# A transposed tile's source moved out of the product buffers, one layernorm reordered and one attention step put a unit later, in a two-layer transformer kernel

## The chip, the cores and the metric

The kernel runs on one core of a Trainium2 chip. The metric is the time on the device in microseconds (us); lower is better. The profiler's span is about 1.7 us shorter than the timed run it belongs to (1243.4 against 1245.1 us for the profile of before), so spans are compared with spans and times with times.

Names of engines: PE is TensorE (matmuls), DVE is VectorE, ACT is ScalarE, POOL is GpSimd, SP issues most of the transfers. The granted clock is the share of TensorE's full clock that the chip let it have, in a stretch of time or as the mean of a run. PSUM is where the matmuls write their results (the `psum` tiles of the kernel), `rstd` is one over a row's standard deviation, and the zero halo is a block of zeros that stands in for the rows above the first.

## The reference

Two layers, each an attention block and a dense block, on x of 2048 rows and 1024 columns in bfloat16:

```python
x = x + A(layernorm(x))     # qkv; attention; @ wo
x = x + B(layernorm(x))     # gelu(x @ w1 + b1) @ w2 + b2
x = x + A(layernorm(x))
x = x + B(layernorm(x))
```

The attention has 32 heads of 32 columns. Each row looks at eight rows only: itself and those 2, 4, ... 14 above it. So the logits are no matmul of q with k: VectorE multiplies q with eight shifted views of k, and a matmul with a matrix of ones and zeros sums the products over each head's columns (a "head sum").

## The kernel before

The rows are worked in four groups of 512. A group's layernorm output `xn` is transposed into `xnT`, on PE for group 0 and by transfers (DMA transposes) for the others. Then come q, k and v in eight chunks of columns each. One chunk is eight matmuls and is called a unit here: units 0 to 7 make q, 8 to 15 make k, 16 to 23 make v. Work that belongs to other stages is hung in at a numbered unit (`sides=at(unit, ...)`).

The part that matters is the start, where the rotation of buffers is filled for the first time. Everything named "big" shares three buffers of 8 KB per partition: the warm-up operand, `xn` of groups 1 and 2, and then the products of q and k.

```python
bigp = ctx.enter_context(tc.tile_pool(name="bigp", bufs=3))
...
def ln_early(n, pool=None):           # layernorm of groups 1 and 2
    xa[n] = new_xnT(pool)
    xns = bigp.tile([P, NTT, D], BF16, name="big")
    ...
        ln_norm(n * NTT + tt, *s[tt], xns[:, tt, :])
        sp.dma_start_transpose(xa[n][:, tt, :, :], xns[:, tt, :]...)
...
def new_prod(n, c):                   # q times shifted k, then pairwise sums
    prod = bigp.tile([P, W, T], BF16, name="big")
    vec.tensor_tensor(out=prod[:], in0=s["qT"]..., in1=win(s["kT"]...), op=ALU.mult)
    ... # after every second product: add two; after every fourth: once more
...
def ln_first():                       # layernorm of group 0
    stats[0] = ln_stats(0)
    stats[1] = ln_stats(1)
    norm(0)
    norm(1)
    stats[2] = ln_stats(2)
    stats[3] = ln_stats(3, between=lambda: norm(2))  # norm(2) between its halves
    norm(3)
...
stage(gen_qkv(0, 2, qk_next=early), sides=... + at(21, head_sum, 0, False))
q1 = gen_qkv(1, 2, defer=True, qk_pool=early)
stage(q1, sides=at(5, attend, 0) + at(5, spread, 0) + at(5, hold) + ...)
```

Group 0 has two head sums. The first (`head_sum(0, False)`, unit 21 of group 0's stage) sums the first four products. The second is the first act of `attend(0)` at unit 5 of group 1's stage: it sums the other four, and the softmax follows. PE takes its instructions in this fixed order, so it waits at a head sum if VectorE is late.

## Time and profile before

| | before |
|---|---|
| time, median of four runs (lowest to highest) | 1243.96 us (1243.51 to 1246.25) |
| the run that the profile shows | 1245.1 us, span 1243.4 us |
| PE busy | 1235.0 us, 99% |
| PE idle, all of it | 8.4 us |

From the page of before, the span, the row of PE's busy time and the shares of the chain that ended last:

```profile
span 1243.4 us, 14103 instructions
PE 1235.0 (99%) x5871; PEld 633.6 (51%) x5871; DVE 836.8 (67%) x864; ACT 305.9 (25%) x477; POOL 94.1 (8%) x215
...
PE 96%; DVE 2%; DMA 1%; SPq 1%; issue 0%; POOL 0%; DVEq 0%
```

PE is the bound, so only its idle time and its slow time can be won. The waits of PE in before (who waited for whom: us in total, times, longest):

```profile
PE L L118 <- DVE big L93: 2.7, 1, 2.7
PE acc L118 <- DVE big L93: 1.1, 1, 1.1
PE acc L118 <- ACT xnT L93: 0.7, 1, 0.7
PE L L217 <- ACT xnT L93: 0.5, 1, 0.5
PE acc L217 <- POOL rstd L93: 0.2, 1, 0.2
```

The longest is one wait of 2.7 us of a head sum (its result is the tile `L`) for the products. The next view, PE's timeline of before, has the columns start, duration, engine, line, operation, tiles, shapes, count and, in brackets, the idle time before and what ended it:

```profile
37.56 12.31 PE L118 MATMUL acc<-xnT,wt 128*128 128x512 bf16 x56
52.58 0.61 PE L118 MATMUL L<-big,smat 128*32 128x512 bf16 x8 [2.72 <-DVE big L93]
53.13 15.72 PE L118 MATMUL acc<-xnT,wt 128*128 128x512 bf16 x64
68.78 0.61 PE L118 MATMUL L<-big,smat 128*32 128x512 bf16 x8
```

The two head sums are at 52.58 and 68.78 us. VectorE's timeline of before shows why the first is late. The third product starts after a wait of 6.33 us for the transposes that read the `xn` in its buffer:

```profile
34.77 2.29 DVE L93 TENSOR_TENSOR big<-big 128x4096 bf16<-128x4096 bf16 x1
43.38 4.50 DVE L93 TENSOR_TENSOR big<-qT,kT 128x4096 bf16<-128x4096 bf16 x2 [6.33 <-DMA xnT<-big]
47.91 4.62 DVE L93 TENSOR_TENSOR big<-big 128x4096 bf16<-128x4096 bf16 x2
...
63.89 4.62 DVE L93 TENSOR_TENSOR big<-big 128x4096 bf16<-128x4096 bf16 x2
```

The last line is the last addition for the second head sum. It ends at 68.51 us, and PE's second head sum starts at 68.78.

The windows view of before gives the busy time of each engine (with its number of instructions), then the granted clock, the share of the DMA engines and GB/s:

```profile
50.00:53.40 3.40, 0.82 (x9) 0.32 (x9) 3.37 (x3) 0.49 (x1) 0.00 (x0) 1.00 1.05 395
53.40:56.80 3.40, 3.40 (x9) 1.34 (x8) 3.40 (x2) 0.15 (x1) 0.00 (x0) 0.50 0.22 82
56.80:60.00 3.20, 3.20 (x16) 2.16 (x15) 3.06 (x3) 1.59 (x4) 0.00 (x0) 1.00 0.36 58
```

From 53.4 to 56.8 us PE works at half clock. Its busy time alone does not show that: it is 3.40 of 3.40 us, but with 9 matmuls in place of about 17. This agrees with the Trainium skill ("Trainium Kernel Development and Optimization", Performance Expectations), which calls the busy time of matmuls a bad metric for how close a kernel is to its roofline.

A smaller stall lies in the first layernorm. ScalarE's timeline of before:

```profile
13.37 0.29 ACT L93 COPY kT<-zhalo 128x112 bf16<-128x112 bf16 x1 [3.21 <-POOL zhalo L93]
13.56 0.28 ACT L93 COPY vT<-zhalo 128x112 bf16<-128x112 bf16 x1
13.75 1.00 ACT L93 COPY xnT<-L 128x1024 bf16<-128x1024 bf16 x1
```

and PE's, at the same place:

```profile
12.34 0.61 PE L217 MATMUL L<-ident,xn 128*128 128x128 bf16 x8
...
14.80 0.61 PE L217 MATMUL L<-ident,xn 128*128 128x128 bf16 x8 [0.53 <-ACT xnT L93]
```

The transposes of tile 2 were done at 12.95 us, but ScalarE stood before a copy of a zero block that GpSimd wrote only at 13.15 us, behind the `rstd` of tile 3. The transposes of tile 3 then waited 0.53 us for ScalarE. The Trainium skill ("TensorE: Matmul & The Clock Gate", Part 1) calls the queues of ScalarE, VectorE and GpSimd strictly first in, first out. The trace agrees: the copy out of `L` starts at 13.75 us, after the two copies of zeros, though its input was ready 0.8 us earlier.

### The profile page before, as it was taken

To read this page: it belongs to the slowest core of one execution; us is meant where nothing else is said; L and a number is where in the kernel's file an instruction comes from. 1 tells how busy PE (TensorE), PEld (TensorE's weight loads), DVE (VectorE), ACT (ScalarE), POOL (GpSimd) and SP (SyncE) were. 2 spreads that over 40 slices of the span, in tenths; PEclk is the share of its full clock that TensorE was granted. 3 is DMA by queue.
4 is the path that set the end of the run, shared out by engine and by line. 5 is a ranking of instruction groups with operands and counts; after the bars stand their busy time and mean duration, and the time that the engine had idled before them with its cause. 6 is when DMAs were issued, how large, how long until landed. Compare 5 with 4: busy or idle time off the path is not lost.

```text
span 1243.4 us, 14103 instructions
## 1 busy us (share of the span) xinstructions
PE 1235.0 (99%) x5871; PEld 633.6 (51%) x5871; DVE 836.8 (67%) x864; ACT 305.9 (25%) x477; POOL 94.1 (8%) x215
## 2 busy tenths in 40 slices
PE   9999999999999999999999999999999999999998
PEld 6566544456444564445644456444554444444444
DVE  7799889996995889427994379943598688012001
ACT  3333152013430134201351013410234101310310
POOL 4010111002001100101000010000000002000000
PEclk9999999999999999999999999999999999999999
DMA  9863564485746557655566565566754567546441
GB/s 283 268 210 138 153 207 148 161 199 182 218 129 205 167 155 201 190 170 147 177 173 197 166 179 166 161 201 194 192 160 141 182 203 196 164 156 195 147 138 55
DMA packets 215328, 219.83 MB, mean 177 GB/s; under 512 B 66066, under 2 KB 184992, under 8 KB 212192
## 3 DMA queue, kind: packets, MB, share of 16 engines
q1 hardware_dynamic: 212592, 208.16, 55.9%
q0 software_dynamic: 2672, 10.76, 2.7%
q8 instruction: 46, 0.75, 0.2%
q14 instruction: 18, 0.15, 0.0%
HBM read 197.40 MB, written 6.29 MB: 164 GB/s over the span
## 4 chain that ended last, share of the span: by engine, by line
PE 96%; DVE 2%; DMA 1%; SPq 1%; issue 0%; POOL 0%; DVEq 0%
PE acc L118 95%; DVE big L93 1%; DVE stats L93 1%; DMA x<-in_A_x_dram 1%; SPq L93 1%; PE L L118 0%; DMA xnT<-big 0%; POOL rstd L93 0%; DVE mv L93 0%; PE acc L217 0%; DVE x L93 0%; DVEq L93 0%
## 5 line engine op out<-in xcount | busy, mean ns | idle before, releaser
L118 PE MATMUL acc<-xnT,wt 128*128 128x512 bf16 (+1 forms) x3376 | 724.1, 377 | 0.7 <-ACT xnT L93 0.7
L118 PEld LDWEIGHTS <-wt 128*128 128x128 bf16 x3376 | 398.4, 119 | 322.4 <-issue 6.4
L118 PE MATMUL acc<-wt,hT 128*128 128x512 bf16 (+1 forms) x1820 | 388.1, 376 | 0.0
L118 PEld LDWEIGHTS <-hT 128*128 128x128 bf16 x1820 | 178.2, 98 | 208.9
L93 DVE TENSOR_TENSOR big<-big 128x2048 bf16<-128x2048 bf16 (+2 forms) x182 | 239.5, 1348 | 1.7
L93 ACT ACTIVATE hT<-acc,b1T 128x512 bf16<-128x512 f32 x224 | 151.6, 687 | 318.5 <-PE acc L118 317.8
L93 DVE TENSOR_TENSOR big<-abc,vT 128x4096 bf16<-128x4096 bf16 x64 | 143.9, 2282 | 49.2 <-DMA abc<-a_d 48.8
L93 DVE TENSOR_TENSOR big<-qT,kT 128x4096 bf16<-128x4096 bf16 x64 | 143.8, 2286 | 30.4 <-ACT kT L93 23.4
L93 DVE TENSOR_TENSOR tmp<-acc,b2bc 128x512 f32<-128x512 f32 x56 | 38.7, 691 | 177.7 <-PE acc L118 173.9
L93 ACT CAST qT<-acc 128x512 bf16<-128x512 f32 x64 | 37.2, 585 | 326.4 <-PE acc L118 326.4
L118 PE MATMUL acc<-wt,oT 128*128 128x512 bf16 x448 | 97.9, 379 | 0.0
L93 DVE BATCH_NORM_STATS2 stats<-x 128x6 f32<-128x512 bf16 x128 | 84.1, 678 | 3.7 <-DMA x<-in_A_x_dram 2.7
L118 PEld LDWEIGHTS <-oT 128*128 128x128 bf16 x448 | 43.8, 98 | 52.9 <-issue 0.2
L93 DVE TENSOR_TENSOR x<-acc,big 128x512 bf16<-128x512 f32 (+1 forms) x9 | 5.7, 632 | 90.0 <-PE acc L118 90.0
L93 ACT CAST vT<-acc 128x512 bf16<-128x512 f32 x64 | 37.5, 586 | 89.3 <-PE acc L118 89.3
L93 ACT CAST kT<-acc 128x512 bf16<-128x512 f32 x64 | 37.5, 585 | 73.0 <-PE acc L118 73.0
L93 POOL TENSOR_TENSOR rstd<-mv,eps_t 128x1 f32<-128x1 f32 x60 | 16.2, 270 | 502.5 <-DVE mv L93 502.5
L93 POOL DMA_DIRECT2D a_d<-a x32 | 18.9, 619 | 411.0 <-DVE a L93 411.0
L93 DVE TENSOR_SCALAR xn<-x,mv,rstd 128x1024 bf16<-128x1024 bf16 x52 | 28.7, 551 | 31.3 <-POOL rstd L93 30.3
L93 DVE TENSOR_TENSOR x<-acc,x 128x512 bf16<-128x512 f32 x64 | 43.0, 672 | 6.7 <-PE acc L118 6.5
L93 DVE TENSOR_TENSOR x<-tmp,x 128x512 bf16<-128x512 f32 x56 | 38.7, 691 | 1.7
L93 POOL TENSOR_TENSOR rstd<-rstd,mhalf 128x1 f32<-128x1 f32 x60 | 33.9, 565 | 4.7
(55 smaller groups left out, 215.6 us busy)
## 6 DMA issues: line engine op xcount, KB each, us to landing
wt<-in_B_w_dram SPq DMA_DIRECT2D x56, 1024.0 KB, 5.8
wt<-in_B_w_dram SPq DMA_DIRECT2D x64, 896.0 KB, 4.9
wt<-in_A_wqkv_dram SPq DMA_DIRECT2D x46, 1024.0 KB, 5.5
wt<-in_A_wo_dram SPq DMA_DIRECT2D x16, 1024.0 KB, 5.0
abc<-a_d POOLq DMA_DIRECT2D x32, 256.0 KB, 4.8
x<-in_A_x_dram SPq DMA_DIRECT2D x16, 256.0 KB, 6.2
out_dram<-x SPq DMA_DIRECT2D x31, 128.0 KB, 1.8
wt<-in_A_wqkv_dram SPq DMA_DIRECT2D x4, 512.0 KB, 7.7
```

The lines of the kernel that those rows point to most:

```text
L93: inst = f(*args, **kwargs)
L118: return pe(nc.tensor.matmul(*args, **kwargs))
```

## The change

The intent: the third group's `xn` (group 2) takes the room of the second group's `qT`, which is not written until PE works on group 1, so that no product waits for group 2's transposes. The first layernorm computes both statistics before it normalises tiles 2 and 3. And `attend(0)` comes one unit later.

```diff
-    def ln_stats(t, mv=None, rstd=None, between=None):
+    def ln_stats(t, mv=None, rstd=None):
 ...
-            if h == 0 and between is not None:
-                between()
 ...
-        stats[3] = ln_stats(3, between=lambda: norm(2))
+        stats[3] = ln_stats(3)
+        norm(2)
         norm(3)
 ...
-        xns = bigp.tile([P, NTT, D], BF16, name="big")
+        xns = bigp.tile([P, NTT, D], BF16, name="big") if pool is None else pool.tile([P, NTT, D], BF16, name="qT")
 ...
-        stage(q1, sides=at(5, attend, 0) + at(5, spread, 0) + at(5, hold) + ...
+        stage(q1, sides=at(6, attend, 0) + at(6, spread, 0) + at(6, hold) + ...
```

## The prediction

> **What bounds the kernel now.** TensorE. The page gives PE 99% busy (1235.0 of 1243.4 us); the chain that ended last is 96% PE. By the timeline, PE's 8.4 us of idle time lies in the first 53 us (1.05 at the start, 0.22, 0.67, 0.53, 2.72) and in a tail of 3.2 us; between them PE never stands still.
>
> **Stall A, 2.72 us, from 49.86.** PE waits for VectorE's first products of group 0 before the first head sum. VectorE is late because its third product waited 6.33 us (37.05 to 43.38) for a product buffer: the waits view says "DMA xnT<-big", the transposes of the third group's xn, which lies in one of the three product buffers. The chain of waits passes through it.
> Afterwards the windows view gives a granted clock of 0.50 from 53.4 to 56.8 us. The casts of vT, otherwise 1.73 us apart, show the eight matmuls after the stall taking 3.45 us and the next eight 1.88: about 1.8 us more lost. The Trainium skill ("TensorE: Matmul & The Clock Gate", Part 1) has PE fall to half clock after an idle window of about 3.4 us and return after a busy one. The trace agrees in length (3.4 us at 0.50), but 2.72 us of idle were enough.
>
> **Stall B, 0.53 us, at 14.27.** The transposes of tile 3 wait for ScalarE's copy of tile 2 out of PSUM. It could have started at about 13.0, but ScalarE's queue first held a copy of the zero halo, which GpSimd wrote only at 13.15, behind the rstd of tile 3, behind VectorE's split statistics.
>
> **What the change does.**
> 1. xn of group 2 moves into the room of group 1's qT, not written before about 55 us; its transposes land by 42.9. The third product then needs only the room of group 1's xn, long transposed, and starts at about 37.1. What ended at 52.5 ends at about 46.2; PE comes at about 49.3. Stall A goes, and its slow clock: -2.72 and -1.8.
> 2. norm(2) ends about 0.35 us later (11.8; PE wants it at 12.2), but tile 3's statistics 0.9 us earlier. The zero halo comes at about 12.3, the PSUM copy ends at about 14.05: stall B goes, -0.5. The next statistics still start at about 13.8, when x lands.
> 3. Attend 0 one unit (1.73 us) later: PE reaches it at about 65.4, not 68.8; VectorE's last add ends at about 62.2, not 68.5. No PE wait; some 4 us idle on VectorE. Softmax and AV of group 0 run 3.4 us earlier, done at about 124.1; PE's wo starts at about 126.7, not 131.8. Slack falls from 4.3 to 2.6 us: still no stall. From the residual adds on, VectorE follows PE, so the whole gain stays.
>
> No work is removed or added; durations stay. All of the gain is on PE's chain: 2.72 + 1.8 + 0.53, about 5.0 us.
>
> **Prediction: 1238.9 us, range 1237.5 to 1241.5.** Faster by over 2%: 1%; within 2%: 98%; slower by over 2%: 1%.
>
> **What would show it.** PE's 2.7 us wait before L gone; no granted clock under 1.0 after 50 us; VectorE's 6.3 us wait on "xnT<-big" gone; PE idle 3.2 to 3.5 us less; span about 1238.4.
>
> **What would make it wrong.** The third product waiting for another buffer (1 to 2 us of stall left); VectorE late at wo or at the late transposes, giving back 1 to 2 us; stall B merely moving; the slow clock returning.

## The result, and the profile after

The changed kernel took 1239.95 us (median of four runs, 1239.72 to 1239.99) against 1243.96 us of before. The ratio is 0.9964, with a 95% interval of 0.9946 to 0.9981. A ratio here is taken over the runs of the same rounds, so it is not quite the ratio of the medians quoted. The gain is 4.0 us in the medians; the two profiled spans differ by 5.2 us.

The page of after:

```profile
span 1238.2 us, 14051 instructions
PE 1230.7 (99%) x5821; PEld 632.5 (51%) x5871; DVE 836.5 (68%) x864; ACT 305.9 (25%) x477; POOL 95.9 (8%) x215
...
PE 99%; issue 0%; ACT 0%; DVE 0%
```

(The 50 matmuls that PE has less are records missing from the trace: the weight loads are 5871 in both, and the two programs have the same number of instructions on PE.) All waits of PE in after:

```profile
PE acc L118 <- DVE big L93: 1.1, 1, 1.1
PE acc L118 <- ACT xnT L93: 0.7, 1, 0.7
```

Both waits, for the head sum and for `xnT` out of `L`, are gone; what is left is the very start and the 0.7 us at 9 us. (The 0.2 us for `rstd` is gone too, but that is no work of the change: this wait runs from nothing to 1.0 us in the profiles, and e5, which has the same layernorm as after, shows the 1.0.) PE's timeline of after has both head sums without a wait, the first 3.6 us earlier:

```profile
48.97 0.62 PE L118 MATMUL L<-big,smat 128*32 128x512 bf16 x8
49.51 15.76 PE L118 MATMUL acc<-xnT,wt 128*128 128x512 bf16 x72
65.20 0.61 PE L118 MATMUL L<-big,smat 128*32 128x512 bf16 x8
```

VectorE's timeline of after: three products in a row from 29.98 us, no wait, the first half sum done at 45.92, the last addition at 61.90, and then 4.21 us of idle time before the softmax:

```profile
29.98 6.69 DVE L93 TENSOR_TENSOR big<-qT,kT 128x4096 bf16<-128x4096 bf16 x3
...
41.30 4.62 DVE L93 TENSOR_TENSOR big<-big 128x4096 bf16<-128x4096 bf16 x2
...
57.28 4.62 DVE L93 TENSOR_TENSOR big<-big 128x4096 bf16<-128x4096 bf16 x2
66.11 1.22 DVE L93 TENSOR_REDUCE mx<-L 128x128 f32<-128x1024 f32 x1 [4.21 <-PE L L118]
```

The windows view of after, the stretch that ran at half clock in before:

```profile
53.40:56.80 3.40, 3.40 (x18) 2.26 (x16) 3.40 (x2) 1.69 (x5) 0.00 (x0) 1.00 0.94 301
```

Twice the matmuls in the same time, at full clock. In the first layernorm, ScalarE's copy out of `L` now starts at 12.85 us and PE's last transposes have no wait:

```profile
12.85 1.01 ACT L93 COPY xnT<-L 128x1024 bf16<-128x1024 bf16 x1
```
```profile
13.97 0.61 PE L215 MATMUL L<-ident,xn 128*128 128x128 bf16 x8
```

### The profile page after: what moved, and what is told of

The parts are those of the page before. It is cut to its first block, busy times and chain, and to the rows that moved or that the text cites. A ratio compares the mean times of both kernels' runs of the same rounds, so it can differ in the third digit from the quotient of the medians.

```text
span 1238.2 us, 14051 instructions
## 1 busy us (share of the span) xinstructions
PE 1230.7 (99%) x5821; PEld 632.5 (51%) x5871; DVE 836.5 (68%) x864; ACT 305.9 (25%) x477; POOL 95.9 (8%) x215
## 4 chain that ended last, share of the span: by engine, by line
PE 99%; issue 0%; ACT 0%; DVE 0%
PE acc L118 99%; PE L L118 0%; PE acc L215 0%; PE L L215 0%; ACT xnT L93 0%; DVE x L93 0%; DVE big L93 0%; PE acc L185 0%
```

## The experiments

Eleven kernels ran. All gave the right result. They went in three batches, each on one chip with nine runs of before beside it, and each kernel was timed in five runs:

| run | what it is | median us (lowest to highest) | ratio to before (95% interval) |
|---|---|---|---|
| batch 1 | before, nine runs | 1243.90 (1243.13 to 1244.64) | |
| e1_before_again | before, unchanged | 1243.86 (1243.32 to 1244.26) | 0.9998 (0.9984 to 1.0011) |
| e2_buffer_only | before + xn in qT's room | 1240.25 (1240.18 to 1240.94) | 0.9971 (0.9959 to 0.9984) |
| e3_norm_only | before + norm(2) later | 1244.11 (1243.17 to 1245.24) | 1.0001 (0.9989 to 1.0014) |
| e4_attend_only | before + attend at unit 6 | 1242.42 (1241.57 to 1244.26) | 0.9990 (0.9977 to 1.0002) |
| batch 2 | before, nine runs | 1244.16 (1242.98 to 1245.24) | |
| e5_after_attend5 | after, attend at unit 5 | 1240.05 (1239.75 to 1240.41) | 0.9968 (0.9954 to 0.9981) |
| e6_halo_early | e2 + zero block written first | 1239.84 (1239.73 to 1240.30) | 0.9967 (0.9954 to 0.9979) |
| e7_before_filled | before + 7 idle-time matmuls | 1244.06 (1243.88 to 1245.35) | 1.0002 (0.9990 to 1.0015) |
| e10_attend_filled | e4 + 7 idle-time matmuls | 1242.26 (1241.56 to 1243.75) | 0.9988 (0.9975 to 1.0000) |
| batch 3 | before, nine runs | 1243.85 (1243.33 to 1244.85) | |
| e11_first_xn_moved | before, the other xn moved | 1243.88 (1242.78 to 1244.72) | 1.0000 (0.9986 to 1.0013) |
| e8_after_u18 | after, first head sum at unit 18 | 1241.83 (1241.53 to 1243.62) | 0.9985 (0.9972 to 0.9997) |
| e9_after_u17 | after, first head sum at unit 17 | 1245.85 (1243.37 to 1245.91) | 1.0010 (0.9997 to 1.0022) |

### e1_before_again: the kernel before once more

No edit. The profile of before was of a run of 1245.1 us, 1.1 us over the median, and the runs of before spread over 2.7 us where those of after lie within 0.3 us.

> The kernel before, unchanged, to see the span and granted clock of each of its runs. Theory: the 2.72 us of idle before the first head sum lets the clock fall, and how long it stays low depends on when the idle falls, so the runs spread over about 1243.4 to 1246.3 us, and a slower run has more microseconds at a clock of 0.50 after 50 us. Rival: the slow clock costs the same 1.8 us each time; then the runs lie within 0.3 us of one another, near 1245.0.

Its runs spread over 0.9 us, and the nine of before beside it over 1.5 us. That looked like the theory; its profile says otherwise. PE's timeline of e1_before_again:

```profile
51.67 0.61 PE L118 MATMUL L<-big,smat 128*32 128x512 bf16 x8 [2.27 <-DVE big L93]
52.22 14.04 PE L118 MATMUL acc<-xnT,wt 128*128 128x512 bf16 x64
67.66 0.62 PE L118 MATMUL L<-big,smat 128*32 128x512 bf16 x8 [1.40 <-DVE big L93]
```

The clock did not fall at this gap (in this trace it fell only in the tail, at 1241.09 us, when PE's last matmul was over). The 64 matmuls took 14.04 us and not 15.72. But PE did not gain by it: it came to the second head sum early and waited there 1.40 us for VectorE. The runs are not faster for having a good clock either: one at 1243.86 us had a mean clock of 0.999, one at 1244.26 us of 1.000. So a second theory was needed. In before, VectorE sets the time up to the second head sum: its third product starts when group 2's transposes have landed, and 25.13 us of products and additions later (43.38 to 68.51 us in the profile of before) PE may go on. How PE spends the time before that, idle or at half clock, hardly matters.

### e2_buffer_only: the room of qT alone

```diff
-        xns = bigp.tile([P, NTT, D], BF16, name="big")
+        xns = bigp.tile([P, NTT, D], BF16, name="big") if pool is None else pool.tile([P, NTT, D], BF16, name="qT")
```

> The kernel before with the third group's xn in the room of qT alone. Theory: the wait of 6.3 us for a product buffer, PE's stall of 2.72 us and the slow clock all go; only the 0.53 us at 14.3 us stays: 1240.5 us, 3.4 to 3.6 us under the median of before. Rival (the gain comes from attend 0 one unit later): 1243.5 to 1244.0.

It came to 1240.25 us, 3.65 us under before. The move of `xn` is nearly the whole gain. Its trace has no wait at either head sum, and VectorE's timeline of e2_buffer_only shows the third product right behind the first two:

```profile
29.65 6.69 DVE L93 TENSOR_TENSOR big<-qT,kT 128x4096 bf16<-128x4096 bf16 x3
```

### e3_norm_only: the layernorm's order alone

```diff
-        stats[3] = ln_stats(3, between=lambda: norm(2))
+        stats[3] = ln_stats(3)
+        norm(2)
```

> The kernel before with norm(2) behind both statistics alone. Theory: PE's 0.53 us at 14.3 us goes, but VectorE's products still end at about 52.5 us, since their wait hangs on the transposes and not on PE; so PE's stall before the head sum grows from 2.72 to about 3.25 us and the time stays that of before, within 0.4 us, apart from the clock. Rival (the parts simply add up): 0.5 us faster than before.

It came to 1244.11 us, no gain. The wait at 14 us is gone from its trace, and PE's wait at the first head sum is 2.77 us (foretold: about 3.25), at the second 1.40 (not foretold). Time won on PE ahead of a wait for VectorE goes into that wait.

### e4_attend_only: attend one unit later alone

```diff
-        stage(q1, sides=at(5, attend, 0) + at(5, spread, 0) + at(5, hold) + ...
+        stage(q1, sides=at(6, attend, 0) + at(6, spread, 0) + at(6, hold) + ...
```

> The kernel before with attend 0 at unit 6, not 5, alone. Theory: no stall of PE is touched (the head sum at unit 5 did not wait for VectorE), so the time stays that of before within 0.4 us. Rival (the move is what gains): 3 us or more faster.

This one surprised: the median is 1.5 us under that of before, though the interval just includes no change. The expectation rested on the profile of before, where the second head sum had no wait. The trace of e4_attend_only shows PE at work on one more unit (72 matmuls between the two head sums and not 64), and then the second head sum at 67.85 us without a wait:

```profile
52.16 15.76 PE L118 MATMUL acc<-xnT,wt 128*128 128x512 bf16 x72
67.85 0.62 PE L118 MATMUL L<-big,smat 128*32 128x512 bf16 x8
```

That fits the second theory: the unit, 1.73 us of work, fills the 1.40 us that e1's run waited.

### e5_after_attend5: after, with attend back at unit 5

```diff
-        stage(q1, sides=at(6, attend, 0) + at(6, spread, 0) + at(6, hold) + ...
+        stage(q1, sides=at(5, attend, 0) + at(5, spread, 0) + at(5, hold) + ...
```

> The changed kernel with attend 0 back at unit 5. The runs so far say that moving it gained 1.5 us in the kernel before, since PE did one more unit of work there before it had to wait for VectorE's last products (second stall, 1.40 us in e1_before_again). New theory: with the free product buffer VectorE is done at about 61.8 us and PE comes at about 63.5, so there is no second stall to hide and the time is that of the changed kernel, 1239.7 to 1240.2 us. Rival (the move gains by itself, whatever the buffer): 1241.4 us.

It came to 1240.05 us, within its own spread of the changed kernel's 1239.95. With the free buffer the last addition ended at 62.42 us and PE arrived at 63.79: nothing is left to hide. This part of the change is worth about 1.5 us alone (by the medians; the interval of e4 just includes nothing) and about nothing beside the first part.

### e6_halo_early: another way to remove the stall at 14 us

```diff
+    pool.memset(zhalo[:], 0.0)
     ln_first()
     build_constants()          # without that memset
```

> e2_buffer_only with the zero halo written by GpSimd before the first layernorm; the statistics stay split. Theory (the stall at 14 us comes from ScalarE's copy of the zero halo, stuck in front of its copy out of PSUM): the stall goes without touching VectorE, PE shows no wait for ScalarE's xnT copy of L, and the time is that of the changed kernel, 1239.7 to 1240.2 us. Rival (it comes from the late xn of tile 3): the stall of 0.3 to 0.5 us stays and the time is e2's 1240.25.

It came to 1239.84 us. VectorE's order is that of e2 (the statistics still split), yet PE waits no more, and its transposes of tile 3 start at 14.04 us, as PE's timeline of e6_halo_early shows:

```profile
14.04 0.61 PE L216 MATMUL L<-ident,xn 128*128 128x128 bf16 x8
```

So the zero block in ScalarE's queue, and not the late `xn` of tile 3, made the stall. The gain over e2, 0.4 us in the medians of two batches, is about that of reordering the layernorm (0.3 us from e2 to after, also of different rounds), and both are at the limit of what these runs resolve.

### e7_before_filled and e10_attend_filled: the clock kept up

```diff
+    def keep_warm(count):
+        ps = acc_tile()
+        for _ in range(count):
+            mm(ps[:], lhsT=ident[:], rhs=ident[:].unsqueeze(1).to_broadcast([P, NTT, P]), start=True, stop=True)
...
-    ... + at(21, head_sum, 0, False))
+    ... + at(21, keep_warm, 7) + at(21, head_sum, 0, False))
```

Seven matmuls of no use fill part of PE's idle time ahead of the first head sum. e7 does so in before, e10 in e4.

> The kernel before with seven matmuls of no use (1.5 us) in front of the first head sum, in PE's idle time, so that the clock stays up. New theory (the time of before is set by VectorE: start of the third product + 25.1 us + what follows; the slow clock only fills time in which PE would wait at the second head sum): no gain, 1243.1 to 1244.7 us as before, with a second stall of 1 to 2 us at about 66 us. Old theory of the prediction (the slow clock adds 1.8 us): runs at 1243.2 at most, and the slow ones gone.

> e4_attend_only with the same seven matmuls. There the second head sum comes one unit later and hides nothing, so a fall of the clock would cost its full 1.7 us (e4's one run of 1244.26 us had a mean clock of 0.999, the others 1.000 and 1241.57 to 1242.95). Theory: with the idle time filled no run has the low clock: all runs 1241.4 to 1243.0. Rival (the low clock comes from the load of the transfers and VectorE, not from PE's idle time): one in three or so runs still at about 1244.2 with a mean clock of 0.999.

All ten filled runs have a mean clock of 1.000, while some unfilled ones of before in every batch have 0.999. Still e7 gains nothing, 1244.06 us. By itself that proves little, since most unfilled runs kept their clock too: of the 27 runs of before beside the three batches, 22 have a mean of 1.000. (Ten filled runs out of ten may also be chance.) But the five with 0.999 took 1244.31 us in the mean and the other 22 took 1243.97: 0.35 us apart, where a slow clock that is paid in full would make it 1.7. PE's timeline of e7_before_filled shows the time come back as the second wait:

```profile
49.93 1.67 PE L118 MATMUL acc<-ident 128*128 128x512 bf16 x7
51.56 0.61 PE L118 MATMUL L<-big,smat 128*32 128x512 bf16 x8
52.11 14.04 PE L118 MATMUL acc<-xnT,wt 128*128 128x512 bf16 x64
67.55 0.62 PE L118 MATMUL L<-big,smat 128*32 128x512 bf16 x8 [1.40 <-DVE big L93]
```

e10 partly missed: its clock held, as expected, but two runs came to 1243.41 and 1243.75 us, over the 1243.0 that was foretold. They were not the profiled runs, so that their transposes landed late is likely and not shown.

### e11_first_xn_moved: as many free buffers, but not the one

```diff
-def ln_early(n, pool=None):
+def ln_early(n, pool=None, xn_pool=None):
-        xns = bigp.tile([P, NTT, D], BF16, name="big")
+        xns = bigp.tile([P, NTT, D], BF16, name="big") if xn_pool is None else xn_pool.tile([P, NTT, D], BF16, name="qT")
-            ln_early(1)
+            ln_early(1, xn_pool=qk_next)
```

> The kernel before, but with the second group's xn in the room of qT, and the third group's left in a product buffer: as many product buffers are free as in e2_buffer_only, but the one left holds the xn whose transposes land last. Theory (what counts is the landing of the third group's transposes): the third product still waits until about 42 to 43 us, and the time is that of before, 1243.1 to 1245.3 us. Rival (any product buffer more is enough): 1240.3 us as in e2.

It came to 1243.88 us, the time of before, with the wait still there in VectorE's timeline of e11_first_xn_moved:

```profile
41.35 4.49 DVE L93 TENSOR_TENSOR big<-qT,kT 128x4096 bf16<-128x4096 bf16 x2 [4.89 <-DMA xnT<-big]
```

So the gain of e2 is not one of having a product buffer more. It is that no product stands in line behind the transposes that land last.

### e8_after_u18 and e9_after_u17: what the slow clock costs where nothing hides it

```diff
-    ... + at(21, head_sum, 0, False))
+    ... + at(18, head_sum, 0, False))      # e9: at(17, ...)
```

In the changed kernel VectorE has time to spare before the second head sum. Moving the first head sum forward in PE's order makes PE idle there for a chosen time, and what it loses is not hidden later.

> The changed kernel with the first head sum three units earlier in PE's order (unit 18, not 21), to put an idle time of known length into it where no second stall hides the clock: VectorE's half sum ends at about 45.9 us, PE comes at 43.8, so PE idles about 2.1 us: 1242.0 us where the clock stays up; about 1243.7 in runs where it falls for 3.4 us (mean clock 0.999). Theory[...]: a mixture, mostly 1242.0. Rival (VectorE's lateness alone sets the time): 1239.95, since the second head sum is not late.

> As e8_after_u18, at unit 17: PE idles about 3.8 us. Theory: idle time[...] lets the clock fall in most or all runs: 1243.8 + 1.7 = 1245.5 us with a mean clock of 0.999, and 1243.8 in any run where it does not. Rival (idle time of this length is not what lets it fall): 1243.8 in all runs with a clock of 1.000.

In e8 the profiled run idled 1.55 us and kept its clock. Four runs came to 1241.53 to 1242.17 us, and one to 1243.62 us with a mean clock of 0.998. In e9 the profiled run idled 3.88 us. Four of its runs had 0.999 and 1245.54 to 1245.91 us, and one had 1.000 and 1243.37 us. PE's timeline of e8_after_u18:

```profile
45.59 0.61 PE L118 MATMUL L<-big,smat 128*32 128x512 bf16 x8 [1.55 <-DVE big L93]
46.14 20.94 PE L118 MATMUL acc<-xnT,wt 128*128 128x512 bf16 x96
```

PE's timeline and the windows view of e9_after_u17:

```profile
46.50 0.61 PE L118 MATMUL L<-big,smat 128*32 128x512 bf16 x8 [3.88 <-DVE big L93]
47.05 24.36 PE L118 MATMUL acc<-xnT,wt 128*128 128x512 bf16 x104
```
```profile
47.55:50.95 3.40, 3.40 (x10) 1.31 (x8) 3.40 (x3) 0.59 (x1) 0.00 (x0) 0.50 1.05 396
```

Here the clock is charged in full. At e8's pace (96 matmuls in 20.94 us) the 104 matmuls of e9 would have taken 22.7 us and not 24.36, so 1.7 us went to the clock, and PE then found VectorE long done at the second head sum (62.30 against 71.33 us). The unprofiled runs fit this: runs with a low clock are about 1.8 us slower in e8 (1243.62 against a mean of 1241.80) and 2.4 us in e9 (a mean of 1245.80 against 1243.37, a single run whose idle time is not known). Half a clock for 3.4 us accounts for 1.7 us of either; what the rest in e9 is, no run shows.

### One sum for all profiles

If everything after the second head sum of group 0 is PE at full speed, then span minus the start of that head sum must be the same in all profiles, except for one unit (1.73 us) less where attend is at unit 6. It is, within 0.4 us:

| profile | last addition ends | second head sum starts | unit | span | span minus start |
|---|---|---|---|---|---|
| before | 68.51 | 68.78 | 5 | 1243.4 | 1174.6 |
| e1_before_again | 67.61 | 67.66 | 5 | 1242.2 | 1174.5 |
| e3_norm_only | 67.80 | 67.85 | 5 | 1242.4 | 1174.6 |
| e7_before_filled | 67.50 | 67.55 | 5 | 1242.4 | 1174.9 |
| e11_first_xn_moved | 66.48 | 66.53 | 5 | 1241.1 | 1174.6 |
| e2_buffer_only | 61.98 | 63.85 | 5 | 1238.5 | 1174.7 |
| e5_after_attend5 | 62.42 | 63.79 | 5 | 1238.4 | 1174.6 |
| e6_halo_early | 62.09 | 63.55 | 5 | 1238.1 | 1174.6 |
| e4_attend_only | 67.54 | 67.85 | 6 | 1240.7 | 1172.9 |
| e10_attend_filled | 67.37 | 67.73 | 6 | 1240.5 | 1172.8 |
| after | 61.90 | 65.20 | 6 | 1238.2 | 1173.0 |
| e8_after_u18 | 61.40 | 67.02 | 6 | 1239.8 | 1172.8 |
| e9_after_u17 | 62.30 | 71.33 | 6 | 1244.2 | 1172.9 |

The upper five are held by VectorE: the head sum starts 0.05 us after the last addition. In the profile of before it is 0.27 us, so there PE, slow by its clock, came last by some 0.2 us. The next three are held by PE, which comes 1.4 to 1.9 us after VectorE is done. In e4 and e10 the two come within 0.4 us of each other. The third product started at 43.38 us in before and at 42.48, 42.66, 42.37 and 41.35 in the other four that wait, so from profile to profile the time of these kernels follows the moment at which the transposes have landed. By the traces the last one landed at 42.86 us in before and at 41.94, 42.54, 41.85 and 41.23 in the others, 0.1 to 0.5 us ahead of the product. (In e7, e4 and e10 the timeline names a cast of vT by ScalarE as what ended the product's wait. It only came last: the product does not read vT, and in e2 it starts at 34.05 us, before any cast of vT.) That the runs without a profile spread for the same reason is likely, since those of after, where nothing on PE's path waits for the transposes, lie within 0.3 us.

## Why the prediction was right, and where it was not

The time was 1239.95 us, inside the range of 1237.5 to 1241.5 and 1.05 us over the point. The forecast of "within 2%" held.

**Stall A, the wait of 2.72 us.** Right, with its cause. The third product waited for the transposes of group 2; with `xn` elsewhere the half sum ends at 45.92 us (foretold: about 46.2) and PE has no wait at 48.97 (about 49.3). e2 shows that this part alone brings 3.65 us, and e11 that it is this buffer and no other.

**The slow clock, "-1.8".** This is the step that failed. The prediction said "All of the gain is on PE's chain: 2.72 + 1.8 + 0.53, about 5.0 us". Along PE's chain of the one run that the profile shows, this sum holds: there PE came to the second head sum 0.27 us after VectorE's last addition, and the change took all of PE's delays away. What failed is the 1.8 as a cost of the kernel. Most runs do not have it: 22 of 27 runs of before had a mean clock of 1.000. In e1, which kept its clock, PE's waits are 2.27, 1.40 and 0.31 us, 4.0 in all: in place of the slow clock there is a second wait of 1.40 us for VectorE, which the prediction did not see. Nor is the slow clock a cost of its own: without it PE would have waited for VectorE instead and gained some 0.2 us of the 1.8, and the runs of before with a low mean clock are 0.35 us slower than the others, not 1.8. The sum that holds for every run is a difference of two arrivals at the second head sum: the later of VectorE and PE before, against the same after.

**The size.** By that sum the run in the profile had 5.3 us to win (68.78, against 63.47, which is after's 65.20 less one unit of 1.73), and the spans did differ by 5.2. But the profile showed a late run: its time of 1245.1 us stood in the same table as the median of 1243.96. In e1's profile, of a run of 1243.94 us, the same sum is 67.66 less 63.47, or 4.2 us, and the medians differ by 4.0. So the prediction's 5.0, taken from one late run, was the right total for that run and 1.0 too much for the median. The range of 1237.5 to 1241.5 us was wide enough for either sum, so that the time fell inside it says nothing for the 1.8.

**Stall B, "-0.5".** The mechanism was right: e6 removes the stall by the zero block alone. The size stays open: from e2 to after the medians of different rounds differ by 0.3 us, no more than these runs resolve, where the profile had 0.53 (in the profiles with the split statistics and the late zero block this wait runs from 0.3 us in e2 to 1.0 in e7). It counts only once stall A is gone, as e3 shows.

**Attend one unit later, said to cost and to bring nothing.** True beside the free buffer (e5, 0.1 us). It was not seen that in before alone it would bring about 1.5 us in the medians (e4); the cause is the same second wait that the prediction missed. VectorE's last addition came at 61.90 us (foretold: 62.2), PE at 65.20 (65.4), its idle time 4.2 us (some 4), and PE's output projection started at 126.50 (126.7) without a stall.

What stays open is why the landing of the last transpose varies by 1.6 us between the five profiles of the table's upper rows, and why the third product starts 0.1 us after it in some and 0.5 us in others. What lets the clock fall is worked out below.

## What to carry to other kernels

When one engine waits twice for the same late engine, the first wait is not the price of the lateness. Follow the late engine to the last place where it is waited for, and take the difference of arrivals there; a slow clock or a saved microsecond upstream of that place counts only as far as it changes which of the two comes last, and when. Check too that the profiled run is a typical one before adding up its microseconds, and where a buffer in a rotation has a slow reader, such as a DMA transpose, see which writer's turn falls on its room, and take that tile out of the rotation. Freeing another buffer did nothing here (e11); a fourth buffer was not tried.

## What the Trainium skill lacked or had wrong

- "TensorE: Matmul & The Clock Gate", Part 1, lets PE fall to half clock after at least one idle window of about 3.4 us, and its section on HAM oscillation (HAM is the page's name for what gates the clock) asks for no idle gaps over about 3.4 us. It does not say how much work a window may hold and still count as idle, and here a gap of 2.72 us was enough (before) while one of 2.27 us was not (e1). The clock records of the 13 kept traces settle it. All 15 falls lie on a grid of 3.413 us, counted from the first clock record of the trace, which agrees with the page's free-running window. Each fall ends a stretch of this grid in which PE was busy at most 1.37 us: 0.79 in before (49.96 to 53.38 us), 1.04 in e9 (44.12 to 47.54), 1.37 in the tail of e8 (1235.29 to 1238.70). No stretch with 1.57 us or more was followed by a fall: 1.57 in e1 (49.83 to 53.25), 1.86 in e8 (44.04 to 47.45). So a window that was busy for 40% of its time still counted as idle, and where a gap lies on the grid decides whether it costs the clock.
- The same section does not warn that the fall can come when PE is already at work again: it came about 0.8 us after PE had started again in before, and about 1.05 us after in e9, so that the first matmuls after a gap are fast and the later ones slow.
- The same page's section "Terms" puts the penalty at about the throttled time times the share of the clock that is lost, here 3.4 us times one half, or 1.7 us. That holds where nothing downstream hides it: 1.7 us in e9's trace. It does not hold where PE would next wait for another engine: in before, runs with a mean clock of 0.999 were 0.35 us slower than those with 1.000.
- "DMA: Bandwidth & Descriptors", in its section on the DMA transpose, states constraints and no time to landing for a transpose between tiles of the on-chip memory (elsewhere the page has a bandwidth for it). In the trace of before the eight transposes of 128x1024 took 3.1 to 10.2 us from issue to landing, 4.3 in the median, and the landing of the last moved by 1.6 us between the profiles in which a product waited for it (41.23 to 42.86 us).
